# Layer 1's chunks 1 to 3 by seven products, with sums chained in PSUM and one plan for all passes

## The chip, the cores and the metric

The kernel runs on one core of a Trainium2 chip. The metric is the device time of one execution in microseconds (us). TensorE (PE) does the matrix products into PSUM, which has 8 banks of 128 partitions x 512 fp32 numbers; VectorE (DVE) and ScalarE (ACT) read and write PSUM and SBUF; GpSimd (POOL) does some work on SBUF; SyncE (SP) issues the DMAs. Each engine runs its own instructions in order and waits on semaphores for the others.

## The reference

Attention over 2 x 8 heads of 768 tokens (a local band beside pooled blocks), then two MLPs on all 1536 tokens, in fp32:

```python
x = attention(q, k, v)                            # 1536 tokens x 512
h = x @ w_in                                      # 512 -> 2048
x = (np.maximum(h, 0.0) + alpha * np.minimum(h, 0.0)) @ w_out     # layer 1
h = x @ w_in2
out = (h * (1.0 / (1.0 + np.exp(-h)))) @ w_out2                   # layer 2
```

## The kernel before

**Precision.** Every fp32 factor is held as a high and a low part in float32r: ACT rounds the high part (a CAST), DVE subtracts it to get the low one. `three` (L289 to L295) multiplies such factors by three matmuls into one PSUM bank: low x high, high x low, high x high (L292, L293, L294).

**Tiles and passes.** The tokens are three tiles of 512. The 2048 features of a layer are four chunks of 512, so there are eight passes: layer 1's chunks 0 to 3, then layer 2's. A pass has *in-products* (for a token tile and each of 4 feature groups, 4 k-steps of three matmuls: 48 matmuls of 512 columns a tile), the *activation* of each group (layer 1: ACT computes m from the bank at L346, DVE g at L352; layer 2: ACT computes Silu at L343; then ACT casts gh, L358, and DVE gl, L361), and *out-products*: 12 items of 4 feature groups x three matmuls, one bank each. The out-products of the four chunks add up in SBUF: `follow1` copies chunk 0's bank to `y` by ACT and adds later chunks by DVE (`y += ps`: L421 and L423 in layer 1, L434 in layer 2). After the last chunk, layer 1's `y` becomes layer 2's `xh` and `xl` (L427, L428).

**Seven products.** In layer 2, token tiles 0 and 1 of each chunk go by Winograd's form of Strassen's scheme: `quad_item` (L218 to L280) computes seven products of half the k-steps (7 x 2 x 3 = 42 matmuls) for feature groups q and q+2 and both tiles, where the direct way takes 48. There are two such chains (q = 0, 1) in a chunk. `combine` (L178) makes the sums of weights and `combine_x` (L197) those of `y`. Each product gets a PSUM bank of its own, and DVE adds the products up on copies in SBUF (`add`, L252).

**What sets the order.** Attention and layer 1's chunk 0 are ordered by `plan()` (L915 to L993) and issued under `manual_schedule`: a step has an engine, a cost, what it comes after, the rooms it takes and gives back, and a due key. From layer 1's chunk 1 on, the order is the list `seq` (L697 to L722): products, then out items, with DVE's and ACT's work behind each item and weight conversions (`convert`) between. PSUM is split in 5 banks for in-products (`ps_mm`) and 3 for out items (`ps_o`). Weights come by 58 DMAs through SP; each is unpacked by three DVE operations (L151, L155, L158), cast by ACT (L164), and its low part made by DVE, in chunk 0 partly by POOL (L167).

Of the kernel before, what the change touches and what calls it, by code (L numbers as in the profile page):

```python
# [10 lines left out]
F32 = mybir.dt.float32  # L11
# [10 lines left out]
P = 128  # L22
# [10 lines left out]
NQ = 6  # L33
# [7 lines left out]
AHEAD, AT_NEXT = 2, 3.58  # L41


@with_exitstack
def tile_blocks_attention_mlps(
# [52 lines left out]
    passes = [(l, c) for l in range(2) for c in range(NCH)]  # L98

# [12 lines left out]
    through = [-1]  # L112
    through_in = [-1]
    through_q = [-1]
    at_load, at_conv = [0], [0]

    def load_next():
        n = at_load[0]
        if n == len(parts):
            return  # L120
# [6 lines left out]
        at_load[0] += 1  # L127

    def conv_next():

        if at_conv[0] == len(parts):
            return None
        i, part, f = parts[at_conv[0]]
        if i < LAST0:
            free = i <= through[0] + 2
        elif part:

            free = i <= through_in[0] + 1 and i <= through[0] + 1 + i % 2
# [12 lines left out]
        nc.vector.tensor_scalar(  # L151
            out=w, in0=high, scalar1=3, scalar2=0x3FFFFFFF,
            op0=ALU.logical_shift_left, op1=ALU.bitwise_and,
        )
        nc.vector.scalar_tensor_tensor(  # L155
            out=w, in0=high, scalar=0xC0000000, in1=w, op0=ALU.bitwise_and, op1=ALU.bitwise_or
        )
        nc.vector.scalar_tensor_tensor(  # L158
            out=w, in0=low, scalar=29, in1=w, op0=ALU.logical_shift_right, op1=ALU.bitwise_or
        )  # L160
        w = w.bitcast(F32)

        def high():
            nc.scalar.copy(out=hi, in_=w)  # L164

        def low(eng=nc.vector):
            eng.tensor_tensor(out=lo, in0=w, in1=hi, op=ALU.subtract)  # L167
            if i > LAST0 and not part:
                w_t[f] = w
                if f >= KT // 2:  # L170
                    combine(i, f - KT // 2)

        return high, low

    def combine(i, kk):  # L178

        half = slice(0, DM // 2), slice(DM // 2, DM)  # L180
        w1_, w2_ = w_t.pop(kk), w_t.pop(kk + KT // 2)
        (a11, a21), (a12, a22) = [[w[:, h] for h in half] for w in (w1_, w2_)]
        nc.vector.tensor_tensor(out=a22, in0=a21, in1=a22, op=ALU.add)
        nc.vector.tensor_tensor(out=a21, in0=a11, in1=a21, op=ALU.subtract)
        nc.vector.tensor_tensor(out=a11, in0=a22, in1=a11, op=ALU.subtract)
        nc.vector.tensor_tensor(out=a12, in0=a12, in1=a11, op=ALU.subtract)

        for n, w in enumerate((w1_, w2_)):
            hi = wpool[1][1].tile([P, 512], F32R, tag="wh", name="sh")
            lo = wpool[1][1].tile([P, 512], F32R, tag="wl", name="sl")  # L190
            sums_t[i, kk, n] = hi, lo
            nc.scalar.copy(out=hi, in_=w)
            nc.vector.tensor_tensor(out=lo, in0=w, in1=hi, op=ALU.subtract)

    tt = []

    def combine_x(kk):  # L197

        t0, t1 = slice(0, TB), slice(TB, 2 * TB)
        k2 = kk + KT // 2  # L200
        b11, b12, b21, b22 = y[:, kk, t0], y[:, kk, t1], y[:, k2, t0], y[:, k2, t1]
        nc.vector.tensor_tensor(out=b11, in0=b12, in1=b11, op=ALU.subtract)
        nc.vector.tensor_tensor(out=b12, in0=b22, in1=b12, op=ALU.subtract)
        nc.vector.tensor_tensor(out=b22, in0=b22, in1=b11, op=ALU.subtract)
        nc.vector.tensor_tensor(out=b21, in0=b21, in1=b22, op=ALU.subtract)

        places = [(tt[0][:, n, 0, kk], tt[0][:, n, 1, kk]) for n in range(3)]
        places.append((xh[:, kk, t1], xl[:, kk, t1]))

        def rest():  # L210
            for (hi, lo), f in zip(places, (b11, b22, b12, b21)):
                nc.scalar.copy(out=hi, in_=f)
                nc.vector.tensor_tensor(out=lo, in0=f, in1=hi, op=ALU.subtract)

        pending.append(rest)
        return lambda: None

    def quad_item(i, q, n, state):  # L218
# [3 lines left out]
        t0, t1 = slice(0, TB), slice(TB, 2 * TB)  # L222
# [26 lines left out]
        def temp(name, pool):  # L249
            return gpool[pool].tile([P, 512], F32, tag="m", name=name, bufs=1 + pool)  # L250

        def add(out, x):  # L252
            nc.vector.tensor_tensor(out=out, in0=x, in1=ps, op=ALU.add)

        def follow():
            if n == 0:
                state["u2"] = temp("u2", 0)
                nc.scalar.copy(out=state["u2"], in_=ps)
            elif n == 1:
                v = temp("v", 1)  # L260
                add(v, state["u2"])
                activate((l, ch, 0, TB, 1), q, 1, [v])
            elif n == 2:
                add(state["u2"], state["u2"])
            elif n == 3:
                state["u3"] = temp("u3", 1)
                add(state["u3"], state["u2"])
            elif n == 4:
                v = temp("v", 1)
                add(v, state["u3"])  # L270
# [8 lines left out]

        return follow  # L280


    pending = []

    def rests():
# [818 lines left out]
```

## Time and profile before

| | |
|---|---|
| timed runs | 595.34, 595.46, 598.3 us (median 595.46) |
| span of the profiled execution | 595.0 us |
| PE busy | 582.1 us (98%), 3571 matmuls |
| DVE busy | 413.9 us (70%), 748 instructions |
| ACT busy | 255.6 us (43%), 587 instructions |
| POOL busy | 54.3 us (9%), 62 instructions |
| DMA moved | 51.02 MB, 86 GB/s over the span |

The profiled execution's own time is not listed beside its span; the timed median lies 0.46 us above that span. Times in the trace are from the span's start. A matmul's record is longer than its share of PE, since matmuls overlap in the array: the pitch, from one start to the next, is what it takes of PE's time.

### The profile page before, as it was taken

The numbers are of one execution on the slowest core, as the hardware profiler recorded it, in microseconds if no ns is written. First come the engines' busy times: TensorE is split into PE (matmuls) and PEld (weight loads), VectorE is DVE, ScalarE is ACT, GpSimd is POOL, SyncE is SP. The second block draws the span as 40 slices with busy tenths as digits, with TensorE's granted clock in tenths as the row PEclk, the third lists the DMA queues.
The fourth block names the chain that finished last, engine by engine and source line by source line (L and its number), as shares of the span: only waits on it lengthen the run. The fifth ranks groups of instructions, "written<-read, shape, count | busy, mean of one in ns | idle before, by whom it ended". The sixth has DMA issues, their size and how long they took to land.

```text
span 595.0 us, 9142 instructions
## 1 busy us (share of the span) xinstructions
PE 582.1 (98%) x3571; PEld 489.1 (82%) x3571; DVE 413.9 (70%) x748; ACT 255.6 (43%) x587; POOL 54.3 (9%) x62
## 2 busy tenths in 40 slices
PE   8899899999999999999999999999999999999997
PEld 6778788999888888888888888888888888888886
DVE  4879999658783853447987699865862698847322
ACT  4788976544431421323444555635512154315210
POOL 2446645200000000000000000000000000000000
PEclk9989999999999999999999999999999999999999
DMA  9957843203440220004220013250220032200111
GB/s 250 275 180 246 232 139 107 73 1 141 142 140 3 66 76 1 0 2 141 72 71 1 0 36 106 84 170 31 65 78 1 4 138 70 72 0 2 71 72 71
DMA packets 23515, 51.02 MB, mean 86 GB/s; under 512 B 2224, under 2 KB 11696, under 8 KB 23472
## 3 DMA queue, kind: packets, MB, share of 16 engines
q1 hardware_dynamic: 23472, 50.44, 27.0%
q8 instruction: 28, 0.46, 0.3%
q14 instruction: 15, 0.12, 0.1%
HBM read 47.29 MB, written 3.15 MB: 85 GB/s over the span
## 4 chain that ended last, share of the span: by engine, by line
PE 87%; DVE 6%; DMA 5%; issue 1%; SPq 0%; ACT 0%; DVEq 0%
PE ps L292 28%; PE ps L293 28%; PE ps L294 28%; DMA y<-in_w 2%; DMA vs<-in_vw 1%; DVE nm L610 1%; PE o L656 1%; DVE t L599 1%; PE pt L639 1%; DMA cst<-in_consts 1%; DVE w L155 1%; DMA kT<-in_kT 1%; PE sc L587 1%; PE pv L536 1%; DVE g L352 1%
## 5 line engine op out<-in xcount | busy, mean ns | idle before, releaser
L292 PE MATMUL ps<-xh,wl 128*128 128x512 f32 (+1 forms) x352 | 127.9, 363 | 0.5 <-POOL wl L167 0.5
L293 PE MATMUL ps<-xl,wh 128*128 128x512 f32 (+1 forms) x352 | 126.7, 360 | 0.0
L294 PE MATMUL ps<-xh,wh 128*128 128x512 f32 (+1 forms) x352 | 126.7, 360 | 0.0
L361 DVE TENSOR_TENSOR gl<-g,gh 128x512 fp32r<-128x512 f32 x91 | 62.9, 692 | 34.2 <-ACT gh L358 34.0
L293 PE MATMUL ps<-gl,wh 128*128 128x512 f32 (+1 forms) x240 | 82.5, 347 | 0.0
L294 PE MATMUL ps<-gh,wh 128*128 128x512 f32 (+1 forms) x240 | 82.3, 346 | 0.0
L292 PE MATMUL ps<-gh,wl 128*128 128x512 f32 (+1 forms) x240 | 79.8, 348 | 0.6 <-ACT pT L370 0.5
L292 PEld LDWEIGHTS ps<-xh,wl 128*128 128x128 f32 x352 | 66.4, 189 | 11.8 <-POOL wl L167 1.0
L293 PE MATMUL ps<-wl,gh 128*128 128x512 f32 (+1 forms) x196 | 75.4, 385 | 0.0
L358 ACT CAST gh<-g 128x512 fp32r<-128x512 f32 x96 | 59.2, 620 | 37.0 <-DVE g L352 34.0
L294 PE MATMUL ps<-wh,gh 128*128 128x512 f32 (+1 forms) x196 | 74.9, 385 | 0.0
L292 PE MATMUL ps<-wh,gl 128*128 128x512 f32 (+1 forms) x196 | 74.9, 385 | 0.0
L294 PEld LDWEIGHTS ps<-xh,wh 128*128 128x128 f32 x352 | 66.4, 189 | 10.0
L293 PEld LDWEIGHTS ps<-xl,wh 128*128 128x128 f32 x352 | 66.4, 189 | 9.9
L421 DVE TENSOR_TENSOR y<-ps,y 128x512 f32<-128x512 f32 x48 | 32.4, 688 | 44.8 <-PE ps L294 44.6
L346 ACT ACTIVATE m<-ps 128x512 f32<-128x512 f32 x48 | 28.6, 596 | 81.4 <-PE ps L294 81.2
L164 ACT CAST wh<-w 128x512 fp32r<-128x512 f32 x64 | 39.3, 621 | 42.5 <-DVE w L158 23.6
L352 DVE SCALAR_TENSOR_TENSOR g<-m,nal,ps 128x512 f32<-128x512 f32 (+1 forms) x60 | 37.2, 637 | 19.7 <-ACT m L346 18.3
L292 PEld LDWEIGHTS ps<-gh,wl 128*128 128x128 f32 x240 | 45.3, 189 | 6.7 <-ACT pT L370 0.7
L293 PEld LDWEIGHTS ps<-gl,wh 128*128 128x128 f32 x240 | 45.4, 189 | 5.8
L294 PEld LDWEIGHTS ps<-gh,wh 128*128 128x128 f32 x240 | 45.3, 189 | 5.6
L294 PEld LDWEIGHTS ps<-wh,gh 128*128 128x128 f32 x196 | 36.8, 188 | 7.4
(90 smaller groups left out, 831.7 us busy)
## 6 DMA issues: line engine op xcount, KB each, us to landing
raw<-in_w SPq DMA_DIRECT2D x58, 512.0 KB, 3.5
vs<-in_vw SPq DMA_DIRECT2D x16, 288.0 KB, 5.4
kT<-in_kT SPq DMA_DIRECT2D x8, 480.0 KB, 6.0
q<-in_qT SPq DMA_DIRECT2D x24, 128.0 KB, 4.3
y<-in_w SPq DMA_DIRECT2D x6, 512.0 KB, 5.0
out<-y SPq DMA_DIRECT2D x11, 256.0 KB, 2.0
raw<-in_vT SPq DMA_DIRECT2D x4, 384.0 KB, 4.1
cst<-in_consts SPq DMA_DIRECT2D x1, 348.0 KB, 4.6
```

The costliest lines, as they stand in the source:

```text
L155: nc.vector.scalar_tensor_tensor(out=w, in0=high, scalar=0xC0000000, in1=w, op0=ALU.bitwise_and, op1=ALU.bitwise_or)
L164: nc.scalar.copy(out=hi, in_=w)
L292: i = nc.tensor.matmul(ps, all_, bh, start=first, stop=False, skip_group_check=again)
L293: nc.tensor.matmul(ps, ah, bl, start=False, stop=False, skip_group_check=again)
L294: nc.tensor.matmul(ps, ah, bh, start=False, stop=last, skip_group_check=again)
L346: nc.scalar.activation(out=m[:, j * w:(j + 1) * w], in_=ps, func=AF.Relu, scale=-1.0)
L352: nc.vector.scalar_tensor_tensor(out=g[:, at], in0=m[:, at], scalar=nal[:, f + j:f + j + 1], in1=ps[:, j * n % w:j * n % w + n], op0=ALU.m ...
L358: nc.scalar.copy(out=gh, in_=g)
L361: eng.tensor_tensor(out=gl, in0=g, in1=gh, op=ALU.subtract)
L421: nc.vector.tensor_tensor(out=at, in0=src, in1=at, op=ALU.add)
L536: nc.tensor.matmul(pt[:NB, :P], band[:rows, odd, at:at + NB], t[:rows, n], start=n == 0, stop=n == NSUB - 1,)
L587: nc.tensor.matmul(ps[s * SUB:(s + 1) * SUB, h, i * NC:(i + 1) * NC], q_[hp, i * P + s * SUB:i * P + (s + 1) * SUB], k_[hp, w0:w0 + NC], s ...
```

## The change

Layer 1's chunks 1 to 3 take the seven products too, on token tiles 1 and 2, while tile 0 stays direct (chunk 0 stays direct on all tiles). For each of these chunks the in-products are 84 + 48 matmuls in place of 144, so 36 matmuls of 512 columns go in all. Attention and chunk 0 keep their matmuls. `x_first` builds the sums of layer 1's inputs from `xh` + `xl` on DVE, and `rebuild` those weights of chunk 1 that were already split.

The products of a chain now add up in PSUM, in both layers. Product 0 goes to bank a. ACT copies bank a to bank c (`seed_c`); product 1 goes on in c; products 2, 3 and 4 go on in a; products 5 and 6 in bank b. Before the bank is written on, ACT keeps a copy of it in SBUF where its value is still wanted (`keep`: u after product 2, v after product 5). DVE's adds within a chain fall from seven to two. In each pass the two chains' products take turns, by the tuple in `quads`.

The out items of chunks 1 to 3 of both layers no longer end in a DVE add: before the item ACT copies `y` into its bank (`out_seed`), all matmuls of the item add to that (`start=False`), and behind it ACT copies the bank back (`out_back`). In the last chunk of layer 1 ACT casts `xh` from the bank, except for the tiles and rows that first go through sums.

All passes are steps of one plan with due times (`put`, `pe`, `late`); seeds are ordered up to LOOK = 3 PE items ahead. The eight banks are one pool. A bank may be seeded by ACT only once it has been wholly written by PE ("mm=").

In numbers over the program: PE 3571 to 3535 matmuls (the 36); DVE 73 adds into `y` fewer (2 of them half as wide), 28 product adds fewer, and sums of x and w and low parts more, 750 to 713; ACT 73 seeds of out items, 14 seeds of bank c, 20 more u and v copies and 67 more copies from banks to `y`, 493 to 687; SP's 133 instructions stay, with the same 58 weight loads; POOL 67 to 69.

PE where chunk 1's in-products begin. Before, tile 0 direct, an item of 12 matmuls in a bank of its own:

```order
L294 MATMUL ps_2305<-xh_78,wh_1606 128x512
L292 MATMUL ps_2336<-xh_78,wl_1381 128x512
L293 MATMUL ps_2336<-xl_79,wh_1380 128x512
L294 MATMUL ps_2336<-xh_78,wh_1380 128x512
L292 MATMUL ps_2336<-xh_78,wl_1488 128x512
```

After, in the first pair of chains (ps_2452 and ps_2467 are the banks a of q = 0 and q = 1, ps_2475 is bank c of q = 0; tt, sh and sl are sums of x and of w):

```order
L298 MATMUL ps_2467<-xh_75,wl_1517 128x512
L299 MATMUL ps_2467<-xl_76,wh_1516 128x512
L300 MATMUL ps_2467<-xh_75,wh_1516 128x512
L298 MATMUL ps_2475<-xh_75,wl_1599 128x512 [waits Activation_49]
L299 MATMUL ps_2475<-xl_76,wh_1598 128x512
L300 MATMUL ps_2475<-xh_75,wh_1598 128x512
L298 MATMUL ps_2475<-xh_75,wl_1641 128x512
L299 MATMUL ps_2475<-xl_76,wh_1640 128x512
L300 MATMUL ps_2475<-xh_75,wh_1640 128x512
L298 MATMUL ps_2452<-tt_2053,sl_2428 128x512 [waits DVE_49]
L299 MATMUL ps_2452<-tt_2053,sh_2427 128x512
```

Product 1 of a chain now waits for ACT's seed, with the six matmuls of the other chain's product 0 between; product 2 goes on in bank a.

ACT where layer 1 ends and layer 2 begins. Before:

```order
L358 CAST gh_3664<-g_3663 128x512 [waits DVE_49]
L346 ACTIVATE m_3687<-ps_3671 128x512 [waits PE_49,Activation_49]
L212 CAST tt_2234<-y_80 128x512 [waits DVE_49]
L258 COPY u2_3723<-ps_3716 128x512 [waits PE_49]
L212 CAST xh_78<-y_80 128x512 [waits DVE_49]
L358 CAST gh_3685<-g_3684 128x512 [waits DVE_49]
L343 ACT_TABLE_LOAD
```

After (ps_3952 and ps_3966 are the banks a of layer 2's first two chains, ps_3974 and ps_3984 their banks c):

```order
L445 CAST xh_75<-ps_3908 128x512 [waits PE_49]
L162 CAST wh_3961<-w_3862 128x512
L244 CAST xh_75<-y_77 128x512 [waits DVE_49]
L286 COPY ps_3974<-ps_3952 128x512 [waits PE_49]
L244 CAST xh_75<-y_77 128x512 [waits DVE_49]
L286 COPY ps_3984<-ps_3966 128x512 [waits PE_49]
L341 ACT_TABLE_LOAD
L341 ACTIVATE g_3996<-ps_3974 128x512 [waits PE_49]
```

The seeds of bank c stand behind casts that wait for DVE's sums of `y`, and PE's product 1 waits for the seeds; the table load of Silu stands behind the two seeds.

The sums of the out items. Before, on DVE:

```order
L423 TENSOR_TENSOR y_80<-ps_3357,y_80 128x512 [waits PE_49]
L423 TENSOR_TENSOR y_80<-ps_3373,y_80 128x512 [waits PE_49]
L183 TENSOR_TENSOR w_3609<-w_3553,w_3609 128x256 [waits DVE_49]
L428 TENSOR_TENSOR xl_79<-y_80,xh_78 128x512 [waits Activation_49]
L423 TENSOR_TENSOR y_80<-ps_3389,y_80 128x512 [waits PE_49]
```

After, on ACT:

```order
L438 COPY y_77<-ps_3202 128x512 [waits PE_49,Activation_49]
L417 COPY ps_3286<-y_77 128x512
L438 COPY y_77<-ps_3232 128x512 [waits PE_49,Activation_49]
L417 COPY ps_3307<-y_77 128x512
L162 CAST wh_3309<-w_3290 128x512 [waits DVE_49]
L438 COPY y_77<-ps_3245 128x512 [waits PE_49,Activation_49]
L417 COPY ps_3326<-y_77 128x512
```

The copy back of one item and the seed of an item three further on take turns in ACT's queue.

The core of the diff:

```diff
+NMM, T_LATER, MM = 5, 150.0, 0.2268
+A_PS, A_SB, D_TT, D_STT, D_HALF = 0.5, 0.53, 0.61, 0.69, 0.36
+EARLY, LOOK = {}, 3
+NEAR, T_NEAR = {"PE": 0.5, "DVE": 0.2, "ACT": 0.15}, 100.0
...
     conv = ctx.enter_context(tc.tile_pool(name="conv", bufs=2))
-    wp0 = ctx.enter_context(tc.tile_pool(name="wp0", bufs=2 * CF))
-    wp1 = ctx.enter_context(tc.tile_pool(name="wp1", bufs=CF))
-    ps_mm = ctx.enter_context(tc.tile_pool(name="ps_mm", bufs=5, space=bass.MemoryType.PSUM))
+    wpool = ctx.enter_context(tc.tile_pool(name="wpool", bufs=3 * CF))
+    ps_mm = ctx.enter_context(tc.tile_pool(name="ps_mm", bufs=1, space=bass.MemoryType.PSUM))
...
+    QUADS = 1
 
     parts = [
         (i, part, f)
         for i, (l, _) in enumerate(passes)
         for part in range(2)
-        for f in ((0, 2, 1, 3) if l and not part else range(CF))
+        for f in ((0, 2, 1, 3) if i > QUADS and not part else range(CF))
     ]
...
+    def x_first(kk, j):
+        t0, t1 = pair(0)
+        k2 = kk + KT // 2
+        if j == 0:
+            for n, tag in enumerate(("wh", "wl", "wh")):
+                x_t[kk, n] = wp2[0].tile([P, TB], F32, tag=tag, name="b")
+        b11, b12, b22 = [x_t[kk, n] for n in range(3)]
+        (add, less, less, add, less, less, less, add)[j](*(
+            (b12, xh[:, kk, t1], xl[:, kk, t1]),
+            (b11, b12, xh[:, kk, t0]),
+            (b11, b11, xl[:, kk, t0]),
+            (b22, xh[:, k2, t1], xl[:, k2, t1]),
+            (b12, b22, b12),
+            (b22, b22, b11),
+            (b11, xh[:, k2, t0], b22),
+            (b11, b11, xl[:, k2, t0]),
+        )[j])
+
...
-        ps = ps_mm.tile([P, 512], F32, tag="mm", name="ps")
+        new = n in (0, 5)
+        if new:
+            st["ab"[n // 5]] = bank()
+        ps = st["acaaabb"[n]]
         for kk in range(KT // 2):
-            three(ps, *ops(kk), kk == 0, kk == KT // 2 - 1)
...
-            elif n == 1:
-                v = temp("v", 1)
-                add(v, state["u2"])
-                activate((l, ch, 0, TB, 1), q, 1, [v])
-            elif n == 2:
-                add(state["u2"], state["u2"])
...
+            three(ps, *ops(kk), new and kk == 0, kk == KT // 2 - 1, not new)
+
+    def seed_c(st):
+        st["c"] = bank()
+        nc.scalar.copy(out=st["c"], in_=st["a"])
+
+    def keep(st, to, at):
+        st[to] = temp(to)
+        nc.scalar.copy(out=st[to], in_=st[at])
+
+    def add_to(st, to, at):
+        add(st[to], st[to], st[at])
...
-            if ch == 0:
-                nc.scalar.copy(out=at, in_=src)
-            elif not last:
-                nc.vector.tensor_tensor(out=at, in0=src, in1=at, op=ALU.add)
...
+    def out_seed(u, m, h, halves):
+        ps = out_ps[u, m, h] = bank()
+        nc.scalar.copy(out=ps[:, :u[3] // halves], in_=out_at(u, m, h, halves))
...
+            first = i == 0 and not seeded
+            if l == 0:
+                three(ps[:, :n], (hi[:, c], lo[:, c]), g_, first, i == CF - 1, seeded)
...
+    def out_back(u, m, h, halves):
+        nc.scalar.copy(out=out_at(u, m, h, halves), in_=out_ps[u, m, h][:, :u[3] // halves])
...
-            items = quad(i, 0)[2:] + quad(i, 1)
-            items.append((n0, in_item, u2, 0))
-            items += [(n0, out_item, u0, m) for m in range(KT)]
...
+        def pe(name, n, after, f, *a, take=(), give=(), key=None):
+            cost = n * MM
+            if key is None:
+                after = [*after, *line[-LOOK:][:1]]
+                line.append(name)
+            put(name, "PE", cost, after, f, *a, take=take, give=give, key=clock[0] if key is None else key)
+            if key is None:
+                clock[0] += cost
+
...
+            after = (
+                lows(i, 0, low) + x_ready(i, ta, low),
+                lows(i, 0, high) + x_ready(i, ta, high) + [at("C")],
+                sl(0) + xs(1) + [at("C")],
+                sl(0) + xs(2) + [at("U")],
+                lows(i, 0, high) + xs(3) + [at("vv")],
+                sl(1) + xs(0),
+                sl(1) + x_ready(i, tb, high) + [at("V")],
+            )[n]
...
+            pe(me, 3 * KT // 2, [*after, "open"], product, i, q, n, st, take=["mm+"] * (n in (0, 5)), give=give)
+            if n == 0:
+                put(at("C"), "ACT", A_PS, [me], seed_c, st, take=["mm="])
+            elif n == 1:
+                act(i, ta, q, me, lambda: st["c"], ("mm", at("C"), 0))
+            elif n == 2:
+                put(at("U"), "ACT", A_PS, [me], keep, st, "u", "a", take=["tmp"])
+            elif n == 3:
+                put(at("vv"), "DVE", D_TT, [me, at("V")], add_to, st, "v", "a")
+                act(i, tb, q + 2, at("vv"), lambda: st["v"], ("tmp", at("V"), 0))
+            elif n == 4:
+                act(i, ta, q + 2, me, lambda: st["a"], ("mm", at("P", 0), 0))
+            elif n == 5:
+                put(at("V"), "ACT", A_PS, [me], keep, st, "v", "b", take=["tmp"])
+            else:
+                put(at("uu"), "DVE", D_TT, [me, at("U")], add_to, st, "u", "b", give=[("mm", at("P", 5), 0)])
+                act(i, tb, q, at("uu"), lambda: st["u"], ("tmp", at("U"), 0))
...
+                put(("Y", *me), "ACT", A_SB / halves, [*ready, "open", *line[-LOOK:][:1]], out_seed, u, m, h, halves, take=["mm="])
...
+            due = clock[0] + 3.0
+            to_x = last and l == 0 and (m >= KT // 2 or t != 1)
...
+            if back:
+                war = [("xs", 1, kk, n) for kk in range(KT // 2) for n in range(4)] if l and c == 0 else []
+                put(("yb", *me), "ACT", A_PS / halves, [done, *war], out_back, u, m, h, halves, give=free, due=due)
...
+            if to_x:
+                put(("Xh", t, m), "ACT", A_PS, [done, *old_in(i)], x_next_high, u, m, due=due)
+                put(("Xl", t, m), "DVE", D_TT, [("Xh", t, m)], x_next_low, u, m, give=free, due=due)
...
+        def quads(i, f=None, *a):
+            for x in ((0, 0), (1, 0), (0, 1), (0, 2), (0, 5), (0, 3), (1, 1), (1, 2),
+                      (0, 6), (0, 4), (1, 5), (1, 3), (1, 6), (1, 4)):
+                if f and x == (1, 5):
+                    f(*a)
+                quad(i, *x)
...
+                    ends = [late(x) for x in after_of.get(name, ())] + [due] * (due is not None)
+                    key = min(ends) - cost - (4.5 if name[0] == "W" else 0.12) - EARLY.get(name[0], 0.0)
...
+            def slots(r):
+                kind = r.rstrip("+=")
+                return sorted(
+                    (x for x in hold[kind] if r != "mm=" or x[1] in whole), key=lambda x: x[0]
+                )
...
+                    if r == "mm":
+                        whole.discard(x[1])
+                    elif r == "mm+":
+                        whole.add(x[1])
```

## Rows read from the trace of the kernel before

**Rows 1.** The page: the span, and each engine's busy time.
```profile
span 595.0 us, 9142 instructions
...
PE 582.1 (98%) x3571; PEld 489.1 (82%) x3571; DVE 413.9 (70%) x748; ACT 255.6 (43%) x587; POOL 54.3 (9%) x62
```

**Rows 2.** Busy time by stretch: length, PE, PEld, DVE, ACT, POOL, clock, DMA share, GB/s.
```profile
sum 120.00, PE 110.34 PEld 94.10 DVE 96.50 ACT 85.05 POOL 54.31; mean PE 7.36 PEld 6.27 DVE 6.43 ACT 5.67 POOL 3.62
...
480.00:520.00 40.00, 40.00 (x178) 33.12 (x177) 35.17 (x65) 16.60 (x30) 0.00 (x0) 1.00 0.23 79
...
560.00:595.00 35.00, 31.73 (x152) 26.58 (x150) 8.43 (x13) 3.66 (x6) 0.00 (x0) 1.00 0.20 75
...
sum 475.00, PE 471.73 PEld 394.99 DVE 317.38 ACT 170.50 POOL 0.00; mean PE 39.31 PEld 32.92 DVE 26.45 ACT 14.21 POOL 0.00
```

**Rows 3.** PE timeline near the end: start, duration, engine, line, operation.
```profile
575.78 0.39 PE L292 MATMUL ps<-xh,wl 128*128 128x512 f32 x1
...
577.82 0.39 PE L292 MATMUL ps<-xh,wl 128*128 128x512 f32 x1
```

**Rows 4.** Lines by form, 130 to 590 us: count, busy, mean ns, idle before.
```profile
L361 DVE TENSOR_TENSOR gl<-g,gh 128x512 fp32r<-128x512 f32 x87 | 59.8, 688 | 32.8 <-ACT gh L358 32.5
...
L352 DVE SCALAR_TENSOR_TENSOR g<-m,nal,ps 128x512 f32<-128x512 f32 x36 | 26.8, 745 | 12.5 <-ACT m L346 12.5
...
L151 DVE TENSOR_SCALAR w<-raw 128x512 uint32<-128x512 uint32 x50 | 20.8, 423 | 10.6 <-DMA raw<-in_w 10.4
...
L183 DVE TENSOR_TENSOR w<-w 128x256 f32<-128x256 f32 x8 | 3.4, 420 | 0.1
...
L258 ACT COPY u<-ps 128x512 f32<-128x512 f32 x8 | 4.7, 584 | 0.3 <-PE ps L294 0.2
...
L343 ACT ACT_TABLE_LOAD x1 | 1.3, 1283 | 0.0
```

**Rows 5.** The same view of POOL, over the whole span.
```profile
L167 POOL TENSOR_TENSOR wl<-w,wh 128x512 fp32r<-128x512 f32 x10 | 12.9, 1289 | 17.7 <-ACT wh L164 17.7
```

**Rows 6.** Timelines of DVE and ACT, instructions one behind the other.
```profile
304.42 0.69 DVE L423 TENSOR_TENSOR y<-ps,y 128x512 f32<-128x512 f32 x1
305.02 0.68 DVE L158 SCALAR_TENSOR_TENSOR w<-raw,w 128x512 uint32<-128x512 uint32 x1
...
128.29 1.14 ACT L164 CAST wh<-w 128x512 fp32r<-128x512 f32 x2
```

**Rows 7.** Timelines: PE hands a bank to ACT, and ACT to PE.
```profile
577.59 0.39 PE L294 MATMUL ps<-xh,wh 128*128 128x512 f32 x1
578.02 0.60 ACT L343 ACTIVATE g<-ps 128x512 f32<-128x512 f32 x1 [12.35 <-PE ps L294]
...
90.22 0.58 ACT L370 COPY pT<-pt 120x512 f32<-120x512 f32 x1
...
90.86 0.39 PE L292 MATMUL ps<-gh,wl 128*128 128x256 f32 x1 [0.47 <-ACT pT L370]
```

**Rows 8.** Timeline of the end, PE and DVE.
```profile
590.97 0.28 PE L293 MATMUL ps<-wl,gh 128*128 128x256 f32 x1
...
591.45 0.28 PE L294 MATMUL ps<-wh,gh 128*128 128x256 f32 x1
...
591.77 0.42 DVE L434 TENSOR_TENSOR y<-ps,y 128x256 f32<-128x256 f32 x1 [1.01 <-PE ps L294]
```

**Rows 9.** Busy time by stretch early on, columns as in group 2.
```profile
24.00:28.00 4.00, 1.99 (x19) 1.61 (x16) 2.53 (x7) 0.98 (x3) 0.98 (x1) 1.00 0.88 228
28.00:32.00 4.00, 3.48 (x23) 2.92 (x24) 2.48 (x9) 3.62 (x18) 3.23 (x6) 0.74 0.85 283
...
60.00:70.00 10.00, 8.31 (x142) 6.34 (x134) 9.88 (x24) 9.04 (x39) 6.03 (x8) 1.00 0.92 261
```

More of the change, by code (lines that the diff above doesn't have):

```diff
@@ L178, in combine @@
[L178 to L193, printed above, removed]
@@ new lines, in bits3, with w_high, w_low @@
+    def bits3(n):
+        for j in range(3):
+            bits(n, j)
+    def w_high(n):
+        i, part, f = parts[n]
+        hi = wpool.tile([P, 512], F32R, tag="wh", name="wh")
+        lo = wpool.tile([P, 512], F32R, tag="wl", name="wl")
+        pieces[(*passes[i], part, f)] = hi, lo
+        nc.scalar.copy(out=hi, in_=w_t[n])
+    def w_low(n, eng):
+        i, part, f = parts[n]
+        hi, lo = pieces[(*passes[i], part, f)]
+        eng.tensor_tensor(out=lo, in0=w_t[n], in1=hi, op=ALU.subtract)
@@ L200, in combine_x, with x_again @@
+    def x_again(kk, j):
+        t0, t1 = pair(1)
         k2 = kk + KT // 2
         b11, b12, b21, b22 = y[:, kk, t0], y[:, kk, t1], y[:, k2, t0], y[:, k2, t1]
[L202 to L218, printed above, removed]
+        less(*((b11, b12, b11), (b12, b22, b12), (b22, b22, b11), (b21, b21, b22))[j])
+    def x_source(l, kk, n):
+        if l == 0:
+            return x_t[kk, (0, 2, 1, 0)[n]]
+        t0, t1 = pair(1)
+        k2 = kk + KT // 2
+        return (y[:, kk, t0], y[:, k2, t1], y[:, kk, t1], y[:, k2, t0])[n]
@@ new lines, in out_item @@
+    def out_item(u, m, h, halves, f0, f1, seeded):
+        l, ch, t0, n, _ = u
+        w = n // halves
+        if f0 == 0 and not seeded:
+            out_ps[u, m, h] = bank()
+        ps = out_ps[u, m, h]
+        for i in range(f0, f1):
+            hi, lo = pieces[l, ch, 1, i]
+            g_ = g_t[t0, ch * CF + i, l]
+            c = slice(m * P, (m + 1) * P)
+            first = i == 0 and not seeded
+            if l == 0:
+                three(ps[:, :n], (hi[:, c], lo[:, c]), g_, first, i == CF - 1, seeded)
+            else:
+                e = slice(h * w, (h + 1) * w)
+                three(ps[:, :w], [x[:, c] for x in g_], (hi[:, e], lo[:, e]), first, i == CF - 1, seeded)
@@ new lines, in tile_blocks_attention_mlps, with put @@
+        NT = NTOK // TB
+        num = {x: n for n, x in enumerate(parts)}
+        more, found_at = [], {}
+        clock, line = [T_LATER], []
+        def put(name, engine, cost, after, f, *a, take=(), give=(), due=None, key=None, size=0):
+            found_at[name] = len(more)
+            more.append([name, engine, cost, list(after), f, a, take, give, due, key, size])
+        def pe(name, n, after, f, *a, take=(), give=(), key=None):
[6 more added lines that the diff above has]
+                clock[0] += cost
@@ new lines, in count, with lows, x_ready, unit @@
+        def count(group, total, entries):
+            return [("#", group, total, entries)]
+        def lows(i, part, fs=range(CF)):
+            return [("lo", num[i, part, f]) for f in fs]
+        def x_ready(i, t, ms=range(KT)):
+            if passes[i][0]:
+                return [("Xl", t, m) for m in ms]
+            return [("x", t * (TB // QB) + b, m) for b in range(TB // QB) for m in ms]
+        def unit(i, t):
+            return (*passes[i], t * TB, TB, 1)
+        def n_outs(i, t):
+            return KT + KT // 2 * ((i, t) in SPLIT) + ((i, t) == END)
@@ new lines, in tile_blocks_attention_mlps @@
+        for n in range(3 * CF, len(parts)):
+            i, part, f = parts[n]
+            summed = not part and i > 1
+            for j in range(3):
+                put(("c", n, j), "DVE", D_HALF if j == 0 else D_TT,
+                  [("W", n)] + ([("c", n, j - 1)] if j else [("c", n - 1, 2)] * (n > 3 * CF) + [("sl", 1, KT // 2 - 1, 1)] * (n == 4 * CF)),
+                  bits, n, j, take=["w"] * (j == 0), give=["raw"] * (j == 2))
+            put(("hi", n), "ACT", A_SB, [("c", n, 2)], w_high, n, take=["wt"])
+            put(("lo", n), "DVE", D_TT, [("hi", n)], w_low, n, nc.vector, give=["w"] * (not summed))
@@ L915, in plan @@
+        for name, e, cost, after, f, a, take, give, due, key, size in more:
+            step(name, e, cost, after, late(name), f, *a, take=take, give=give, size=size)
         def plan():
```

630 lines of the change are left out of this document (367 added, 263 removed).

## Prediction

> **What bounds the kernel now.** I read the page's first part, then busy time by stretch, then PE's timeline. PE is busy 98% of the span [rows 1]. By stretch, PE is busy 110.34 of the first 120 us, so 9.66 us of idle lie in attention and chunk 0; from 120 to 595 it is busy 471.73 of 475, and the missing 3.27 us are the same 3.27 that the last stretch alone lacks (31.73 of 35) [rows 2], that is the tail behind the last matmul. So from 120 us on, where the whole change lies, PE never waits, and the time there is the number of matmuls by their pitch. Nine 512-wide matmuls lie between starts at 575.78 and 577.82 [rows 3]: 2.04 / 9 = .2267 us each. DVE is next, at 70%, ACT is at 43% [rows 1]: the change moves work from the first two to the third, and adds places where PE waits for it.
>
> **The sum, part by part.**
>
> *Matmuls.* Three chunks lose 12 matmuls each (84 + 48 against 144): 36 x .2267 = -8.16 us, all on the path, as PE has no gap there to swallow it.
>
> *Units for the rest.* DVE's 512-wide operation has a record of .69 us, but the next starts .60 behind it [rows 6], so the pitch is .09 below the record; by that .745 for g becomes .66, and .42 for half-width and unpacking becomes .33 [rows 4]. Two ACT casts take 1.14, so .57 each [rows 6]. PE's last matmul of a bank (577.59, .39 long, so to 577.98) frees ACT at 578.02, .04 later; an ACT copy that ends at 90.80 frees PE at 90.86, .06 later [rows 7]. A copy out of a bank takes .58 [rows 4].
>
> *Chunk 1's entry.* The weights and inputs are split already, so DVE must form the sums of x and of w while PE does the rest of chunk 0's out items: 126 wide matmuls and 144 half-wide ones (four in .48 us [rows 8], so .12 each): 28.6 + 17.3 = 45.9 us of PE. DVE has 76 instructions before the first product that needs them: 51 wide, 5 g, 20 half-width. By pitch 30.6 + 3.3 + 6.6 = 40.5 us, by full records 35.2 + 3.7 + 8.4 = 47.3. So DVE is between 5.4 early and 1.4 late. DVE at 35.17 of 40 us, 88%, left PE without a gap between 480 and 520 [rows 2], and 40.5 of 45.9 is the same 88%: I take 0.
>
> *Layer boundary.* Layer 2's first product 1 waits for the seed of bank c, and in ACT's queue this seed stands behind a cast of a y sum, which waits for DVE's last combination, the 49th of its instructions since the last out items began. By pitch 41 wide, 2 g and 6 narrow ones are 24.6 + 1.3 + 2.0 = 27.9 us; with the cast .57, the seed .58 and .06 that is 29.1. PE reaches the waiting matmul 120 matmuls on, 27.2 us. So 1.9 us late if DVE starts with no lead, 0 if it is an out item (12 x .2267 = 2.7) ahead, 6.3 late by full records (32.3 + 1.2 - 27.2). Behind the waiting cast stand the second seed and the Silu table load (1.28 [rows 4]); 18 matmuls, 4.1 us, lie before PE needs that bank, about what cast, two seeds, load and Silu take. I take the middle of lead and no lead, 1.0.
>
> *Bank copies within the chains.* Product 1 waits for the seed of c, product 3 for u, product 6 for v, product 4 for DVE's vv. With the two chains taking turns, four of these a pair of chains have only one item of six matmuls between (seed and u of q = 0, v and vv of q = 1), so 28 waits in seven pairs; the others have three items or more. From the start of the last matmul before the copy PE is covered for 7 x .2267 = 1.59 us; the chain is .39 + .04 + .58 + .06 = 1.07 with ACT, 1.18 with DVE's .69. That leaves .52 and .41: one ACT instruction fits ahead, on DVE two thirds of one. From ACT's 43% (it rises: 194 more instructions of .58 make some 368 of 588 us, 63%) an instruction is often ahead, two seldom. Bounds 0 and, at two ahead everywhere, 18.5 (rival C); I take .3.
>
> *ACT writing PSUM.* No row shows it. The nearest, ACT reading PSUM, is .58; the far bound is the slowest 512-wide operation, POOL's 1.29 [rows 5]: chain 1.78, .19 late at the 7 close seeds, 1.3 us. ACT is nearer to ACT: 0.
>
> *Out items.* 73 seeds are ordered three items ahead, 3 x 2.7 us, which covers .58 many times; the copies back take DVE's place and free the bank later only by the queue on ACT. DVE loses 73 adds and 28 product adds, and has no row in which PE waited for it there: 0. The weight loads are the same 58 on SP: 0.
>
> *Tail.* A half-wide DVE add of .42 follows the last matmul [rows 8]; now an ACT copy half as wide. By the rows .1 either way: 0.
>
> Sum: -8.16 + 1.0 + .3 = -6.9. The profiled execution's span is 595.0, and the median timed run 595.46, .46 above it: 595.0 - 6.9 = 588.1, and with the .46, **588.6 us**.
>
> The Trainium skill (page "Perfetto Trace Analysis", section "Optimizing Tensor Performance", Matmuls) says that independent groups of matmuls should rotate through banks, so that ACT or DVE empties one while the next group runs. It speaks against a chain that keeps on in one bank; were no other chain between, each of the 42 seeds and copies would cost 1.07 - .23 = .84, 35 us in all and 624 us. The order puts another chain's six matmuls between, so by the rule too most of it goes, and this is rival C at its far end.
>
> **The rivals.**
>
> A, the forecast: 588.6, own range 587.2 to 590.5.
>
> B, DVE late at the two entries: full records instead of pitches, 1.4 + 6.3 = 7.7 in place of 1.0: 595.3; half of that, 591.9. For it: DVE ran 9.88 of 10 us between 60 and 70 [rows 9], so its pitch can be all there is, and the two entries hold its densest work. Against it: the same density did no harm at 480 to 520 [rows 2].
>
> C, the slower one: the bank copies are late inside the chains. It is one mechanism, ACT's queue in front of a copy that PE waits for: at two instructions ahead, 21 x (1.14 - .52) + 7 x (1.20 - .41) = 13.0 + 5.5 = 18.5, so 588.3 + 18.5 = 606.8. From 8.16 / 28 = .29 us a wait on, the change is slower. For it: ACT was idle only .3 us ahead of all 8 of before's copies u [rows 4], so something usually stood ahead of them in its queue. Against it: by my count ACT stays idle over a third of the time, so the queue is short.
>
> D, the clock: short idles let the granted clock fall. From 24 to 28 us PE was busy 1.99 of 4 and the clock in the next 4 us was .74 [rows 9], a loss of .26 x 4 = 1.04 us; once in each of 14 chains that would be 14.6, so 603.2. Against it: 8.31 busy of 10 kept 1.00 [rows 9]. The Trainium skill ("TensorE: Matmul & The Clock Gate", section "A second HAM failure mode: psum-queue depth-cycling") reports a kernel whose clock swung because PE idled briefly between groups while it cycled through banks; the trace here shows a fall only behind an idle half, so I leave this little.
>
> E, the change doesn't do what it says: matmuls that go on in a bank written by ACT are slower, or the seeds' banks come free too late for three items ahead, and half the gain is gone: 592.7.
>
> **How the numbers follow.** Chances: A .70, B .13, C .09, D .02, E .06. What a measurement can tell from no change is .5%, so faster is below 592.48 and slower above 598.44. Faster: all of A, half of B and of E, .70 + .065 + .03 = .80. Same: the other half of B and of E, .095, and a quarter of C, .12 together. Slower: the rest of C, and D, .08 in round numbers. The range starts at 587.0 (all of -8.16 gives 587.3, a tail .1 shorter and the spread of the timed runs the rest) and goes to 592.8, with half of B and E inside.
>
> **What would show it.** In the profile after: some 36 matmuls fewer and PE's busy time lower by about 8; the same idle of some 9.7 us before 120 us; PE without waits on ACT in chunks 1 to 3, or with ones below .3 us; a gap of up to 2 us where layer 2's first product 1 waits for ACT; DVE clearly below 413.9 us, ACT near 368; the clock at 1.00 from 40 us on. It is wrong if idle on PE from 120 us to the end, tail apart, is above 4 us (B where one gap holds it, C where many do), or if the pitch of a matmul that adds to an ACT-written bank is not .2267.

## The result, and the profile after

The changed kernel takes 588.51 us (median of 4 runs, 587.72 to 590.6) against 595.62 for the kernel before beside it: ratio .9875, interval .9847 to .9903. In a later set of runs it was 589.96 against 595.94, ratio .990 (.9881 to .992). The forecast was 588.6, faster: the gain is clear of noise both times, but that the first median lies within .1 us of the forecast is luck, as single runs of the changed kernel go from 587.3 to 591.1.

Its page, span and busy times, answers to [rows 1]:

```profile
span 585.9 us, 9240 instructions
...
PE 573.2 (98%) x3535; PEld 481.2 (82%) x3535; DVE 398.2 (68%) x711; ACT 353.4 (60%) x781; POOL 57.3 (10%) x64
```

36 matmuls fewer, DVE lower, ACT 98 us higher. But PE is 8.9 us less busy and the span 9.1 us shorter, more than 36 matmuls are worth. Part of this is not the change. Each later run lists its span beside its time, 1.8 us apart, so before's profiled execution (595.0) took some 596.8, 1.3 above its median. Its granted clock was .74 from 28 to 32 us [rows 9] and .84 from 32 to 36, where the changed kernel's profile has 1.00; that is (.26 + .16) x 4 = some 1.7 us by estimate. (A clock of 1.00 is the level of 2.4 GHz; a stretch below it was partly at 1.2 GHz.) First before, then the changed kernel:

```profile
32.00:36.00 4.00, 4.00 (x61) 2.79 (x60) 1.96 (x5) 2.67 (x6) 2.11 (x3) 0.84 0.18 65
```

```profile
28.00:32.00 4.00, 4.00 (x47) 3.33 (x46) 2.06 (x8) 3.84 (x18) 3.48 (x7) 1.00 0.80 286
32.00:36.00 4.00, 3.92 (x65) 3.32 (x65) 3.97 (x8) 3.77 (x13) 1.44 (x2) 1.00 0.22 72
```

The part of the program that the change touches begins with the first 512-wide matmul, so I measure from there to the start of the last matmul (the *stretch*). Here is its start before (it ends at 591.45, [rows 8]), then the changed kernel's two ends; the columns are those of [rows 3]:

```profile
127.88 0.50 PE L292 MATMUL ps<-xh,wl 128*128 128x512 f32 x1
```

```profile
125.60 0.50 PE L298 MATMUL ps<-xh,wl 128*128 128x512 f32 x1
...
582.35 0.28 PE L300 MATMUL ps<-wh,gh 128*128 128x256 f32 x1
```

463.57 before, 456.75 after: -6.82 us. Ahead of it the two kernels differ by 2.28, but among all profiles of this study that beginning ends anywhere between 125.2 and 129.6, and the lowest time of before (594.43, span 592.6, so some 125.5 by the same stretch and tail) starts as early as the changed kernel. From the start of the last matmul to the end both have 3.6. So I compare stretches; in a second profile of the changed kernel it was 456.70.

Inside it PE waits once. The waits of PE from 113 us on, then the windows (columns as in [rows 2]):

```profile
PE ps L298 <- ACT ps L286: 0.7, 1, 0.7
```

```profile
120.00:160.00 40.00, 40.00 (x290) 36.82 (x289) 33.99 (x59) 19.66 (x36) 1.62 (x1) 1.00 0.08 27
160.00:200.00 40.00, 40.00 (x179) 33.05 (x178) 37.02 (x64) 27.81 (x52) 0.00 (x0) 1.00 0.19 54
...
320.00:360.00 40.00, 39.35 (x174) 32.03 (x173) 32.91 (x56) 27.74 (x50) 0.00 (x0) 1.00 0.17 47
```

It is the seed of layer 2's first bank c. PE, ACT and DVE there:

```profile
333.45 0.39 PE L300 MATMUL ps<-xh,wh 128*128 128x512 f32 x1
334.49 0.50 PE L298 MATMUL ps<-xh,wl 128*128 128x512 f32 x1 [0.65 <-ACT ps L286]
334.82 0.39 PE L299 MATMUL ps<-xl,wh 128*128 128x512 f32 x1
```

```profile
333.33 0.62 ACT L244 CAST xh<-y 128x512 fp32r<-128x512 f32 x1 [1.07 <-DVE y L170]
333.86 0.58 ACT L286 COPY ps<-ps 128x512 f32<-128x512 f32 x1
```

```profile
331.41 1.28 DVE L170 TENSOR_TENSOR tt<-y,tt 128x512 fp32r<-128x512 f32 x2
332.62 0.68 DVE L170 TENSOR_TENSOR y<-y 128x512 f32<-128x512 f32 x1
```

Read upward from PE: the seed starts when the cast ahead of it has gone; the cast waited 1.07 for a y sum that DVE makes at 332.62. The start at 334.49 is 1.04 behind the one before it instead of .23, and the next again .33: .81 + .11 = .92 us. Twice more a matmul has that pitch of .33 without a listed wait (288.64 behind vv, 338.74 behind u): a sum by DVE and a copy by ACT that came just too late, .12 and .15. Sum: -8.16 + .92 + .27 = -6.97; a pitch longer by .00005 in 1920 matmuls adds .1, which makes -6.87, against the -6.82 measured.

### The profile page after: what moved, and what is told of

The parts are those of the page before. It is cut to its first block, busy times and chain, and to the rows that moved or that the text cites. A ratio compares the mean times of both kernels' runs of the same rounds, so it can differ in the third digit from the quotient of the medians.

```text
span 585.9 us, 9240 instructions
## 1 busy us (share of the span) xinstructions
PE 573.2 (98%) x3535; PEld 481.2 (82%) x3535; DVE 398.2 (68%) x711; ACT 353.4 (60%) x781; POOL 57.3 (10%) x64
## 4 chain that ended last, share of the span: by engine, by line
PE 81%; DVE 10%; DMA 4%; ACT 2%; issue 1%; POOL 1%; SPq 0%; ACTq 0%; DVEq 0%
PE ps L298 26%; PE ps L300 26%; PE ps L299 26%; DVE w L146 2%; DMA vs<-in_vw 1%; DMA y<-in_w 1%; DVE nm L615 1%; DVE t L604 1%; PE o L661 1%; DMA cst<-in_consts 1%; DVE w L140 1%; DVE xl L170 1%; DMA kT<-in_kT 1%; PE pt L644 1%; DVE tt L170 1%
## 5 line engine op out<-in xcount | busy, mean ns | idle before, releaser
L170 DVE TENSOR_TENSOR gl<-g,gh 128x512 fp32r<-128x512 f32 x72 | 48.6, 690 | 89.6 <-ACT gh L349 89.2
L298 PE MATMUL ps<-xh,wl 128*128 128x512 f32 (+1 forms) x292 | 104.8, 359 | 1.3 <-ACT ps L286 0.7
L299 PE MATMUL ps<-xl,wh 128*128 128x512 f32 (+1 forms) x292 | 103.4, 354 | 0.0
L300 PE MATMUL ps<-xh,wh 128*128 128x512 f32 (+1 forms) x292 | 103.4, 354 | 0.0
L438 ACT COPY y<-ps 128x512 f32<-128x512 f32 (+1 forms) x81 | 47.2, 582 | 83.1 <-PE ps L300 82.7
L146 DVE SCALAR_TENSOR_TENSOR w<-raw,w 128x512 uint32<-128x512 uint32 x116 | 82.0, 707 | 3.4
L298 PEld LDWEIGHTS ps<-xh,wl 128*128 128x128 f32 x292 | 55.1, 189 | 10.8 <-POOL wl L167 1.1
L167 DVE TENSOR_TENSOR wl<-w,wh 128x512 fp32r<-128x512 f32 x54 | 37.1, 693 | 22.6 <-ACT wh L162 21.7
L349 ACT CAST gh<-g 128x512 fp32r<-128x512 f32 x72 | 43.5, 621 | 6.5 <-DVE g L335 5.3
L299 PEld LDWEIGHTS ps<-wl,gh 128*128 128x128 f32 x196 | 36.8, 188 | 7.4
```

The source lines that it names most:

```text
L146: nc.vector.scalar_tensor_tensor(out=w_t[n], in0=in0, scalar=scalar, in1=w_t[n], op0=op0, op1=ALU.bitwise_or)
L167: eng.tensor_tensor(out=lo, in0=w_t[n], in1=hi, op=ALU.subtract)
L170: nc.vector.tensor_tensor(out=out, in0=a, in1=b, op=op)
L298: i = nc.tensor.matmul(ps, all_, bh, start=first, stop=False, skip_group_check=again)
L299: nc.tensor.matmul(ps, ah, bl, start=False, stop=False, skip_group_check=again)
L300: nc.tensor.matmul(ps, ah, bh, start=False, stop=last, skip_group_check=again)
```

## The experiments

"Stretch" is as above: 463.57 before, 456.75 changed.

**1. Layer 1 direct again, all else as changed.**

```diff
-        QUAD = {i: i >= 1 for i in range(len(passes))}
+        QUAD = {i: i >= NCH for i in range(len(passes))}
```

(and for passes 1 to 3 tiles 1 and 2 by `direct`, no sums of x and w). 

> Layer 1's chunks 1 to 3 direct on all tiles again; the plan, the seeded out items on ACT and layer 2's chained products stay. Measure: the stretch from the first 512-wide matmul to the last matmul, 463.57 us before and 456.75 after. Theory (the gain is 36 matmuls by their pitch, all else is hidden): 456.75 + 8.16 = 464.9, less the small waits inside layer 1's chains (.1), so 464.8; time some 8 us above the changed kernel, 596.5, no gain over before. Rival (the plan, the ACT seeds or the chaining give part of the gain, the products less): the stretch is well below 463.6, at 461 or less.

Measured: stretch 464.70, ratio to before 1.0022 (.9993 to 1.0051). The plan, the chaining and the ACT seeds without layer 1's products give nothing; the layer boundary's wait is still there (.80), and the stretch is even 1.1 longer than before's.

**2. The chains of a pass no longer take turns.**

```diff
-            for x in ((0, 0), (1, 0), (0, 1), (0, 2), (0, 5), (0, 3), (1, 1), (1, 2),
-                      (0, 6), (0, 4), (1, 5), (1, 3), (1, 6), (1, 4)):
+            for x in ((0, 0), (0, 1), (0, 2), (0, 5), (0, 3), (0, 6), (0, 4),
+                      (1, 0), (1, 1), (1, 2), (1, 5), (1, 3), (1, 6), (1, 4)):
```

> The two chains of a pass no longer take turns: q = 0 runs 0, 1, 2, 5, 3, 6, 4 and then q = 1, so product 1 stands right behind product 0, whose bank ACT must copy first. Theory (the turn of the other chain hides the copy): each of 14 seeds of bank c now costs .39 + .04 + .58 + .06 - .23 = .84 us, 11.8 in all; u, v and vv keep six matmuls between. Stretch 456.75 + 11.8 = 468.5, more where the seed finds something ahead on ACT. Rival one (the seed would be hidden anyway): 457. Rival two (short idles bring the clock down): granted clock below 1.00 behind the 14 idles and over 480.

Measured: 461.46, +4.71, which neither said. The plan, which knows the costs, put another product (5, or the other chain's 4) between in 13 of the 14 places; one bare seed remained, behind a copy of `y` and a cast, and cost 1.68. Of the rest, 1.5 are gh and gl at chunk 1's first out items (192.6 us) and .5 is u at the layer boundary:

```profile
PE ps L298 <- ACT ps L286: 2.2, 2, 1.5
PE ps L298 <- ACT gh L349: 0.7, 1, 0.7
```

An edit of a list is not an edit of the order when a planner stands between.

**3. The same with PE's order fixed to the list.**

```diff
-                after = [*after, *line[-LOOK:][:1]]
+                after = [*after, *line[-1:]]
```

> As e2_chains, but the plan may no longer put other PE items between: PE's items keep the order in which they are listed, so each of the 14 products 1 stands right behind its product 0. Theory (the turn of the other chain hides the copies): at least 14 x .84 = 11.8 us more than the changed kernel's 456.75, 468.5 or above, above it where a seed finds casts ahead on ACT (1.68 at the one bare place that e2 had). Rival one (a copy costs PE far less than its chain of .39 + .04 + .58 + .06): under 461. Rival two (idles bring the clock down): granted clock under 1.00 behind 130 us.

Measured: 484.02, +27.3. All 14 seeds are waited for, with 18.7 us of idle in all: .66 to 1.85 each, and once 4.28. The chain alone leaves .04 + .58 + .06 = .68 of idle; what is above it stood ahead on ACT (at 4.28, the layer boundary, casts that wait for sums of `y`). To the pitch a wait adds its idle, .16 by which records overlap (.39 - .23), and the .11 behind it: 18.7 + 14 x .27 = 22.5 of the 27.3.

```profile
PE ps L298 <- ACT ps L286: 18.7, 14, 4.3
```

Two of the idles are followed by a lower clock. The first (windows):

```profile
210.00:214.00 4.00, 4.00 (x19) 3.34 (x18) 2.93 (x6) 1.43 (x4) 0.00 (x0) 1.00 0.53 150
214.00:218.00 4.00, 2.15 (x9) 1.43 (x9) 3.21 (x6) 1.56 (x3) 0.00 (x0) 0.94 0.60 201
218.00:222.00 4.00, 4.00 (x13) 3.18 (x12) 2.27 (x4) 1.48 (x3) 0.00 (x0) 0.63 0.51 184
```

PE was idle for 1.85 there, and the next stretch has .63: partly at the lower level, where the pitch was .43 in place of .2267. After the longest wait (4.28, from 349.5 us) two stretches had .76 and .81. Behind the other twelve, idle .66 to 1.64, the clock stayed at 1.00. So the cover by the other chain is what the turn buys. What length of idle brings the clock down is not shown: in experiment 5 an idle of 1.90, with PE a little less busy, was followed by 1.00:

```profile
204.00:208.00 4.00, 2.10 (x10) 1.44 (x9) 3.67 (x6) 2.15 (x5) 0.00 (x0) 1.00 0.60 146
208.00:212.00 4.00, 4.00 (x19) 3.32 (x18) 1.93 (x4) 1.70 (x4) 0.00 (x0) 1.00 0.55 179
```

**4. Every bank copy twice.**

```diff
-        nc.scalar.copy(out=st["c"], in_=st["a"])
+        for _ in range(2):
+            nc.scalar.copy(out=st["c"], in_=st["a"])
```

(u and v likewise). 

> Each of the 42 copies of a bank (c, u, v) is made twice, one behind the other, and PE waits for the second; the order is that of the changed kernel. It adds 42 x .49 us to ACT, and at each close copy as much delay as one more instruction ahead in the queue. Theory (a slack of .52 at each close copy, mostly unused): chain .39 + .04 + .49 + .58 + .06 = 1.56 of 1.59, so nothing but where something stands ahead; the layer boundary grows by .5 to 1.0; stretch 457.3 to 459. Rival (the slack is already used up by ACT's queue): 21 x .49 = 10 us more, 467.

Measured: 464.00, +7.25, between the two. The boundary grew by more than forecast: the seed's pitch is over by 1.41 (.81 in the changed kernel), u's by 1.06 (.04). The main error was the price of the second copy: two take 1.2, so it adds .62 and not .49, and the chain becomes .39 + .04 + 1.21 + .06 = 1.70, against a cover of 1.59. PE is late at all 21 close copies by ACT (seed and u of q = 0, v of q = 1, in seven pairs) and at one vv, and nowhere else. At 16 of these 22 no wait is listed: PE is .06 to .16 late, and the next pitch is .11 over as well, 3.4 us in all. Here is one, with the copies that it follows:

```profile
175.98 0.39 PE L302 MATMUL ps<-tt,sh 128*128 128x512 f32 x1
176.31 0.50 PE L300 MATMUL ps<-tt,sl 128*128 128x512 f32 x1
176.64 0.39 PE L301 MATMUL ps<-tt,sh 128*128 128x512 f32 x1
```

```profile
175.04 1.21 ACT L292 COPY u<-ps 128x512 f32<-128x512 f32 x2 [0.27 <-PE ps L302]
```

One more instruction of .62 in front of every copy, then, costs about the whole gain: the cover of 1.59 and the slack of .52 that I worked out are real, and no more than that.

**5. Out seeds ordered behind the item just before theirs.**

```diff
-                put(("Y", *me), ..., [*ready, "open", *line[-LOOK:][:1]], out_seed, ...)
+                put(("Y", *me), ..., [*ready, "open", *line[-1:]], out_seed, ...)
```

> The seeds of out items are ordered behind the PE item just before theirs, not behind the third before it. Theory (the seeds are free only because they are ordered ahead): each of the 73 seeds now lies on PE's path with at least .58 + .06 us, and behind what ACT has queued: 73 x .64 = 47 us more at most, 500; with part of them still started early since no semaphore holds them, some 480. Rival (ACT, 60% busy, runs ahead by itself, so order matters little): under 460.

Measured: 478.64, +21.9, near the theory's 480: 18 listed waits for seeds (14.0 us of idle, and .27 more each, as in experiment 3), u at the layer boundary (.7 of idle), and near misses. Ordering the seeds ahead is what makes them free.

```profile
PE ps L298 <- ACT ps L417: 14.0, 18, 1.9
```

**6. Out items of chunks 1 to 3 added by DVE again** (no seeds, but for layer 1's last chunk).

```diff
-                put(("yb", *me), "ACT", A_PS / halves, [done, *war], out_back, ...)
+                put(("yb", *me), "DVE", D_TT / halves, [done, *war, *ready], out_sum, ...)
```

> The out items of chunks 1 to 3 are added to y by DVE again (one add of .69 each in place of ACT's seed and copy back), except layer 1's last chunk, which keeps its seeds; 61 instructions more on DVE, 122 fewer on ACT. Theory (PE's time is its matmuls, and the ACT seeds were only a swap between engines with room): stretch 456.75 +- .5. Rival (DVE, 37 of 40 us busy between 160 and 200 us of the changed kernel, is the next bound and the seeds are what keeps PE fed): DVE late in chunks 1 and 2, stretch 460 or more.

Measured: 456.78, no change, with DVE at 38.23 of 40 us in the window where it had 37.02:

```profile
160.00:200.00 40.00, 40.00 (x178) 32.99 (x177) 38.23 (x66) 18.48 (x33) 0.00 (x0) 1.00 0.13 40
```

**7. All sums in the old manner**: besides, each product in its own bank and seven DVE adds a chain.

```diff
-        ps = st["acaaabb"[n]]
+        ps = st[n] = bank()
```

> Seven products in layer 1 as in the changed kernel, but all sums in the old manner: each product in a bank of its own with seven DVE adds a chain, out items added by DVE (layer 1's last chunk keeps its seeds); 131 instructions more on DVE than in the changed kernel, 150 fewer on ACT. Theory (the gain is the 36 matmuls alone, and DVE has the room: 398 + 131 x .60 = 477 us of 586): stretch 456 to 459. Rival (chaining in PSUM and the ACT seeds are what makes the seven products affordable in layer 1): DVE late in chunks 1 to 3, 465 or more, so that little of the gain is left.

Measured: 459.59, just past the theory's end and far from the rival's: 3.98 of the 6.82 us are left. DVE is nearly full in chunks 1 to 3 (38.1 to 38.3 of 40 us between 160 and 280) and late in two places, where PE waits for gh and then gl at split out items:

```profile
PE ps L298 <- ACT gh L349: 1.9, 2, 1.3
PE ps L299 <- DVE gl L170: 1.1, 2, 0.6
```

By pitch the two places cost 4.1. The waits of the changed kernel at the layer boundary and its near misses (1.2) are gone, as bank c has no seed; so both moves of sums undone cost 2.8 us net. With the chaining, and seeded out items in layer 1's last chunk alone, nothing is lost (6); the seeded out items without the chaining were not run.

**8. Eight more DVE adds at chunk 1's entry.**

```diff
+        for _ in range(8) if (kk, j) == (0, 0) else ():
+            add(b12, xh[:, kk, t1], xl[:, kk, t1])
```

> One DVE add at chunk 1's entry is made eight times more (4.8 us by pitch). Theory (the entry has 5.4 us of room by pitch): hidden, stretch 456.75 to 457.5. Rival (the room is smaller, as DVE is busy 37 of 40 us between 160 and 200, so that the backlog is handed on to the activations of chunk 1): 2 to 5 us more, 459 to 462, by waits for gh and gl at chunk 1's first out items rather than at its products.

Measured: 462.40, +5.65, just past the rival's range: its mechanism, earlier still. The adds stand in DVE's queue ahead of chunk 0's own activations, and PE waits for those from 149 us on (first and third line), not for the sums; the second line is the wait at the layer boundary that the changed kernel has too. Behind the two waits the clock fell, and the .96 of that window is some 1.6 us of the 5.65.

```profile
PE ps L300 <- ACT gh L384: 2.6, 1, 2.6
PE ps L300 <- ACT ps L288: 0.6, 1, 0.6
PE ps L301 <- DVE gl L387: 0.6, 1, 0.6
```

```profile
120.00:160.00 40.00, 36.76 (x268) 34.12 (x267) 33.65 (x56) 17.58 (x32) 1.62 (x1) 0.96 0.07 19
```

**9. The seeds of the layer boundary ahead of the casts**: for the sums that only product 4 reads,

```diff
-    put(("xsh", l, kk, n), "ACT", A_SB, [j_(at[n]), *old, *war, "open"], ...)
+    put(("xsh", l, kk, n), "ACT", A_SB, [j_(at[n]), *old, *war, "open"] + [("C", NCH, 1)] * (n == 3 and l), ...)
```

> At the layer boundary ACT's two casts of the y sums for tile 1 (needed only by product 4) come after the two seeds of bank c. Theory (the one wait of the changed kernel, .65 us plus the restart behind it, is the seed queued behind those casts): the wait goes, the stretch falls by .8 to 1.0 to 455.9. Rival (the seed is late through product 0 or the bank, or the later casts make product 4 or the table load late instead): the stretch stays within .3 of 456.75.

Measured: 456.65. The seed's wait goes, and as long a one appears three products on, at u, which now queues behind the two casts, the table load, Silu and its cast:

```profile
338.67 0.50 PE L298 MATMUL ps<-tt,sl 128*128 128x512 f32 x1 [0.68 <-ACT u L290]
```

```profile
335.58 1.28 ACT L341 ACT_TABLE_LOAD   x1
336.88 0.60 ACT L341 ACTIVATE g<-ps 128x512 f32<-128x512 f32 x1
337.51 0.62 ACT L349 CAST gh<-g 128x512 fp32r<-128x512 f32 x1
338.04 0.58 ACT L290 COPY u<-ps 128x512 f32<-128x512 f32 x1
```

**10. And u ahead of the table load**, by letting the first Silu come after it.

```diff
-            put(("g", *me), "ACT", A_PS, [src], act_silu, ...)
+            put(("g", *me), "ACT", A_PS, [src] + [("U", i, 0)] * (me == (NCH, 0, 0)), act_silu, ...)
```

> e4_seedfirst and the first copy u of layer 2 ahead of the table load and of the first Silu on ACT. Theory (e4 only moved the wait to u, which stood behind the table load, Silu and its cast): both waits go, stretch 456.65 - .84 - .1 = 455.7. Rival (a third instruction is late now: v, the Silu results or vv, since the table load's 1.28 us are spent somewhere in this queue anyway): 456.5 or more.

Measured: 455.60; PE lists no wait from 124 us to the end, and the window of the boundary is full:

```profile
320.00:360.00 40.00, 40.00 (x178) 33.14 (x177) 33.95 (x58) 28.59 (x51) 0.00 (x0) 1.00 0.17 52
```

**11. Both timed together.** This version: 

> The kernel of e8_ufirst, timed. Theory (its stretch, 455.60, is 1.15 us shorter than the changed kernel's, and the rest is the same): 1.1 to 1.2 us below the changed kernel timed beside it, a ratio to it of .998, and to before of .985 to .988. Rival (the 1.15 us are lost in the spread of the first 125 us): no difference of the medians that stands out.

The changed kernel: 

> The changed kernel again, timed beside e9. Theory: 588 to 589 us, a ratio to before of .9875 to .989 (-6.82 us of 595.5 is .9885); stretch 456.75 again, within .1. Rival (the first profile's early start of 2.3 us belongs to the change): its first 512-wide matmul again at about 125.6, well ahead of before's 127.88.

Measured: 588.95 (586.99 to 593.21) and 589.96 (587.3 to 591.06); ratios to before .9898 (.9866 to .9929) and .990 (.9881 to .992). Both ratios to before lie just above their forecasts, as does the changed kernel's time, with intervals that reach into them. The stretches repeat (455.68 and 456.70), the first 512-wide matmul came at 126.66 and 125.22. The 1.0 us between the stretches is shown by the traces; the times alone don't tell it from the spread of the beginning, as the rival had it. The 125.22 is early again, but that does not belong to the change: by listed spans less stretch and tail, the beginning has a median of some 127.0 in 25 executions of before and 127.4 in 10 of the changed kernel (an estimate).

## Why the prediction was right

*Matmuls, -8.16.* Right, and alone the source of the gain (experiment 1).

*Layer boundary, +1.0.* .92, through the cast that was named. The 1.0 was the middle of bounds from 0 to 1.9 (6.3 by records), so its closeness is partly luck. Not named: behind the seed stands a second late instruction, u (.15 here, a wait of .7 once the seed was moved).

*Bank copies, +.3.* .27 in two places, but one of these is the u just named, so the chains themselves lost .12, at one vv; .3 was a choice between 0 and 18.5. The close waits and their slack held (3 and 4). Too generous was "one ACT instruction fits ahead": a cast of .57 is already more than .52, and experiment 4's .62 was late at every close copy. And I left out that a late start has .11 behind it, so a near miss costs more than its lateness.

*Chunk 1's entry, 0.* No wait, but mis-sized: not 5.4 us of room. In the changed kernel the weight sum that product 2's second half needs is done at 167.1 and PE takes it at 169.62, so 2.5 are left there (the first of the two sums is the one that is read):

```profile
166.40 1.29 DVE L170 TENSOR_TENSOR sl<-w,sh 128x512 fp32r<-128x512 f32 x2 [0.28 <-ACT sh L192]
```

```profile
169.62 0.39 PE L298 MATMUL ps<-tt,sl 128*128 128x512 f32 x1
```

And ahead of that the room is smaller, as chunk 0's activations pass through the same queue (8). Adding up DVE's work against PE's over the whole entry hid this.

*ACT writing PSUM, as .58.* It is .574 from bank to bank and .593 from SBUF:

```profile
L417 ACT COPY ps<-y 128x512 f32<-128x512 f32 x71 | 41.8, 593 | 0.0
...
L286 ACT COPY ps<-ps 128x512 f32<-128x512 f32 x14 | 8.0, 574 | 4.6 <-PE ps L300 4.6
```

*ACT's total.* Forecast 368, measured 353.4: 194 instructions take .50 each of busy time, as those in a row overlap; I had used whole records.

*Span.* Forecast 588.1, measured 585.9, though the time was right: I took the .46 between the timed median and the profiled span for the same execution's, when it was two executions with different beginnings.

*Rivals.* B, DVE late, was near: with the old sums it costs 4.1 us at the activations (7), and in the changed kernel the one wait starts from a sum of DVE. C, late copies, is real wherever the cover goes (3, 4). D showed in 3, where two waits were followed by a clock that cost some 3.4 us, and in 8, and in neither profile of the changed kernel. E did not show: the matmuls of out items, most of which now add to a seeded bank, keep a pitch of .2267, and no seed of an out item is waited for. The Trainium skill ("Perfetto Trace Analysis", "Optimizing Tensor Performance") says that independent groups of matmuls should rotate through banks, so that one is emptied while the next runs. The traces agree: with other products between, only one of the 14 seeds is waited for, that of the layer boundary; without them all are, with 18.7 us of idle (3).

What stays open: experiment 7 does not tell how much of its 2.8 us goes to the chaining alone. Nor does any run have seven products in layer 1 under the old order, so what the one plan is worth is not shown.

## What to carry to other kernels

Where PE is full, count matmuls first: 36 of them were the whole gain, and of the rest the moves of sums to ACT kept 2.8 us of it (7), while the seeded out items could be left out at no loss, but for layer 1's last chunk, where both runs keep them (6). Dependent products in one bank are free while another chain's products cover the copy, and the slack must be counted against what stands ahead on the copying engine: here .52 us, so that .62 more was too much. When one wait is moved out of a queue, look for the next instruction in that queue whose reader is as close; only after both had moved was the time won in the traces.

## What the runs showed of the hardware

A matmul that starts late on a semaphore, even with no listed wait, has a record of .50 in place of .39, and the next starts .33 behind it in place of .2267. So a near miss costs .11 us on top of its lateness (16 without a listed wait in experiment 4: 1.66 of lateness and 1.75 behind it).

A copy of 128x512 by ACT into PSUM takes .574 from a bank and .593 from SBUF. Two copies of one bank to the same place, one behind the other, take 1.2.

The granted clock stayed at 1.00 behind twelve idles of .66 to 1.64 (experiment 3) and one of 1.90 (experiment 5), and fell behind idles of 1.85 and 4.28 (3) and behind 2.61 and .63 in a row (8).
